# One transfer per group of ten query rows, on partitions 4 to 123, in an attention and two-layer MLP kernel

## The chip, the cores and the metric

The kernel runs on one core of a Trainium2 chip. The core has a matrix engine (PE, with its weight loads listed as PEld), a vector engine (DVE), a scalar engine (ACT), a general engine (POOL), a queue engine that here only issues transfers (SP), and 16 DMA engines that carry the transfers of all queues. On-chip memory (SBUF) and the matrix engine's result memory (PSUM) both have 128 partitions. The metric is the time of one execution in microseconds (us).

## The reference

Attention with two batches, 12 heads, 448 positions and 64 features per head, in which the heads are mixed before and after the softmax, and then two MLP layers on the 896 x 768 result:

```
scores = scale * q @ k^T
scores = einsum('bhij,hg->bgij', scores, w_pre)
attn = exp(scores - max(scores)) / (sum + 1e-9)
attn = einsum('bhij,hg->bgij', attn, w_post)
x = (attn @ v) laid out as [896, 768]
h = x @ w_in;  x = (h * relu6(h + 3) / 6) @ w_out
h = x @ w_in2; out = (max(h,0) + alpha * min(h,0)) @ w_out2
```

## The kernel before

Queries are cut into eight tiles of 120, 120, 120 and 88 rows per batch. For a tile, `qk` makes the scores of two heads at a time (`sc`), and `s_out` copies them to an SBUF tile `S` with query rows on the partitions and [head, key] along the free dimension. There are two such tiles, one for even and one for odd query tiles, so tile t can only be written once everything of tile t-2 has been read.

Mixing heads needs head and row together on the partitions. So the rows of a tile are taken in groups of ten (90 groups; in a 120-row tile group g has rows g, g+12, g+24, ..., in an 88-row tile the step is 8, and the last 8 rows are a group of their own). `pull` moves a group from `S` to a tile `pull` with 12 x 5 = 60 partitions per five rows: SBUF to SBUF, in pieces of 448 numbers (1792 bytes), one piece for each row and head. Before the change a group is moved by two transfers of five rows each, both to the same half of the partitions (0 to 59 for even groups, 64 to 123 for odd ones), beside each other in the free dimension. The scores lie with the first half of a tile's rows from partition 0 on and the second half from partition 64 on.

Two groups make a pair; there are 45 pairs, and the main loop runs over them. In iteration p: `premix(p)` multiplies the pulled rows with the block-diagonal `wpre` (PSUM tiles `mx`, two buffers) and takes the row maxima on DVE (`nm`); `qk` makes scores of a later tile; `exp(p)` runs on ACT; `s_out` copies the scores; `norm(p)` scales `wpost` on DVE; `post(p-1)` mixes the heads again on PE (`pt`), `post_evac(p-1)` copies the result to `MT` on ACT; `av` multiplies with the values for an earlier tile, and its result goes to `xT`. Near the end of the loop the first weight blocks are loaded and converted (`wst`, `wb`, `whi`, `wlo`) and the first chains of the MLP (`p`) begin.

All the instructions stand in the order of the program on each engine. SP issues, in iteration p, the pulls of the pair p+2 and the loads of queries, keys, values and weights. It waits only for what a transfer needs: the scores of a new tile, a free buffer (four pairs of `pull` tiles, two to four buffers of the others), and a semaphore of which there are eight for all transfers. It can therefore run ahead of the other engines by a pair or more.

From 254.8 us on there is only the MLP: 64 weight blocks, each used by 36 matmuls of 448 columns.

Of the kernel before, what the change touches and what calls it, by code (L numbers as in the profile page):

```python
# [7 lines left out]
F32 = mybir.dt.float32  # L8
# [7 lines left out]
PSUM = bass.MemoryType.PSUM  # L16

Q = 64
EB = 384

W_MIN = 2.0 ** -15
# [13 lines left out]
def kernel(  # L35
# [15 lines left out]
    nc = tc.nc  # L51
    _, D, H, S = k.shape
    B, D = q.shape[0], D // 2
    DM, NT = out.shape
    JP, NJ = v.shape[1], v.shape[3]
    JH = JP // 2
    KF = alpha.shape[0] // 128
    KD = DM // 128
    G = 10
    GP = G * H  # L60
    G2 = G // 2
    GH = G2 * H
    WP = GH
    HC = 3
    scale = 1.0 / float(D) ** 0.5

    tiles = []
    groups = []
    for b in range(B):
        for i0 in range(0, S, GP):  # L70
            n = min(GP, S - i0)
            t = len(tiles)
# [32 lines left out]
    with tc.manual_schedule():  # L105
# [21 lines left out]
        def load_q(ti, c):  # L127
            T = tiles[ti]
            n = T["n"]
            t = q_st[ti, c] = kq.tile([128, HC, GP], F32, tag="qst", bufs=4, name="qst")  # L130
            a = T["i0"] * H + 2 * HC * c * n
            for o in range(2):
                src = q[T["b"], D * o:D * o + D, a:a + 2 * HC * n]
                nc.sync.dma_start(  # L134
                    out=t[D * o:D * o + D, :, :n],
                    in_=src.rearrange("p (j o x) -> p j o x", j=HC, o=2)[:, :, o, :],
                )

# [7 lines left out]

        S_t, MT = {}, {}

        def half(ti):
            return G2 * (tiles[ti]["n"] // G)  # L150

        def qk(ti, j, tag="sc"):
            n, m = tiles[ti]["n"], half(ti)
            if j == 0:
                S_t[ti] = (s_odd if ti % 2 else s_even).tile([128, H, S], F32, tag="S", name="S")
            pool_ = psB if tag == "sc" else psA
            ps = [pool_.tile([128, 512], F32, tag=tag, bufs=2, name="sc") for _ in range(2)]
            t = q_st[ti, j // HC]
            for a, z, r in ((0, Q, 0), (m, n, Q)):
                for o in range(2):  # L160
                    nc.tensor.matmul(  # L161
                        ps[o][r:r + z - a, :S], t[D * o:D * o + D, j % HC, a:z],
                        k_st[tiles[ti]["b"]][D * o:D * o + D, j, :], start=True, stop=True,
                    )
            w = Q + n - m
            return [(S_t[ti][:w, 2 * j + o, :], ps[o][:w, :S]) for o in range(2)]

        d_t, mx_t, e_t, sm_t, wr_t, pt_t = {}, {}, {}, {}, {}, {}

        def pull(g):  # L170
            ti, o, st, xn = groups[g]
            if g % 2 == 0:
                d_t[g // 2] = late.tile([128, 2, S], F32, tag="pull", bufs=4, name="pull")
            r = Q * (g % 2)
            for c in range(2):
                x = min(G2, xn - c * G2)
                a = Q * c + o if st > 1 else Q + o - half(ti) + c * G2
                src = S_t[ti][bass.ds(a, x, step=st)] if st > 1 else S_t[ti][a:a + x]
                nc.sync.dma_start(d_t[g // 2][r:r + x * H, c, :], src)  # L179

        def premix(p):
            d = d_t.pop(p)
            ms = []
            for o in range(2):
                ms.append(psA.tile([128, 512], F32, tag="mx", bufs=2, name="mx"))
            for c in range(2):
                for o in range(2):
                    x = min(G2, groups[2 * p + o][3] - c * G2) * H
                    a = Q * o
                    nc.tensor.matmul(  # L190
                        ms[o][Q * c:Q * c + Q, :S], wpre[a:a + x], d[a:a + x, c, :],
                        start=True, stop=True,
                    )
            nms = []
            for m in ms:
                nm = late.tile([128, 1], F32, tag="nm", bufs=4, name="nm")
                nc.vector.tensor_reduce(nm, m[:, :S], axis=AX.X, op=ALU.max, negate=True)  # L197
                nms.append(nm)
            mx_t[p] = ms, nms
# [33 lines left out]

        def post_evac(p):
            ts = pt_t.pop(p)
            two = [groups[2 * p + o] for o in range(2)]
            for ti, *_ in two:
                if ti not in MT:
                    MT[ti] = late.tile([128, NJ, H, GP], F32, tag="MT", bufs=2, name="MT")
            for c in range(2):  # L240
                s = ts[c][:Q + JH, :2 * NJ * GH].rearrange("p (o u x) -> p u o x", o=2, x=G2)
                if two[0][0] == two[1][0] and two[1][2] > 1:
                    ti, o, _, _ = two[0]
                    d = MT[ti][:Q + JH, :, :, o * G:(o + 2) * G].rearrange("p t g (o x) -> p (t g) o x", o=2)
                    nc.scalar.copy(d[..., c * G2:(c + 1) * G2], s)  # L245
                    continue
                for k_, (ti, o, st, xn) in enumerate(two):
                    x = min(G2, xn - c * G2)
                    r = (o * G if st > 1 else o) + c * G2
                    d = MT[ti][:Q + JH].rearrange("p t g x -> p (t g) x")  # L250
                    nc.scalar.copy(d[:, :, r:r + x], s[:, :, k_, :x])

        def by_row(dst, src, n):
            m = n // G * G
# [145 lines left out]
        def open_late():  # L400
            p_late.close()
            p_xt.close()
            p_ps.close()
            P["ps6"] = pool(ctx, "ps6", bufs=6, space=PSUM)
            P["g1"] = pool(ctx, "g1", bufs=2 * KF - NE)
# [43 lines left out]
        def in_chain(i, xs, c):  # L449
            p = ptile()[:, :S]  # L450
            in_part(p, i, xs, c, 0, KD)
            return p

        def g_tile(f, c):
            return pair(P["g0" if c == 0 and f < NE else "g1"], "g")


        def act1(p, g, f):
            hi, lo = g
            t = P["tmp"].tile([128, S], F32, tag="t", name="t")  # L460
            nc.scalar.activation(out=t, in_=p, func=ACTF.Relu, bias=three)
            yield
            nc.vector.scalar_tensor_tensor(
                out=t, in0=t, scalar=6.0, in1=p, op0=ALU.min, op1=ALU.mult
            )
            nc.scalar.activation(out=hi, in_=t, func=ACTF.Copy, scale=1.0 / 6.0)
            yield
            nc.vector.scalar_tensor_tensor(
                out=lo, in0=t, scalar=1.0 / 6.0, in1=hi.bitcast(F32),
                op0=ALU.mult, op1=ALU.subtract,  # L470
            )
# [13 lines left out]
        def run(a):  # L485
            for _ in a:
                pass
# [28 lines left out]
        load_k0(3, H // 2)  # L516
        for c in range(2):
            a = GH * c
            nc.sync.dma_start(out=wpre[Q * c:Q * c + GH, :GH], in_=w_pre[a:a + GH, a:a + GH])
        load_q(1, 0)  # L520
        for c in range(2):
            a = GH * c
# [3 lines left out]
        nc.gpsimd.tensor_copy(  # L526
            wpost.rearrange("p (g x) -> p x g", g=H), wraw.rearrange("p (x g) -> p x g", g=H)
        )

        def s_out(pairs):  # L530
            for o, (d, s_) in enumerate(pairs):
# [46 lines left out]
        for p_ in range(-2, NP + 1):  # L578
            if p_ == -2:
                for g in range(4):  # L580
                    pull(g)
            elif 0 <= p_ < NP - 2:
                pull(2 * p_ + 4)
            for f in load_at.get(p_, []):
                f()
            for ti, c in load_q_at.get(p_, []):
                load_q(ti, c)
            if 0 <= p_ < NP:
                premix(p_)
            pend = [qk(ti, j, "mx" if p_ < 0 and j == 1 else "sc") for ti, j in qk_at.get(p_, [])]  # L590
            if 0 <= p_ < NP:
                exp(p_)
            for two in pend:
                s_out(two)
            if 0 <= p_ < NP - 2:
                pull(2 * p_ + 5)
            if 0 <= p_ < NP:
                norm(p_)
            if 1 <= p_:
                post(p_ - 1)  # L600
                post_evac(p_ - 1)
            kk = 2 * (p_ - (NP - KD // 2))
            if kk == 0:
                p0 = ptile()[:, :S]
            if 0 <= kk < KD:
                in_part(p0, 0, x_t, 0, kk, kk + 2)
            if p_ == NP:
                p1 = in_chain(1, x_t, 0)
                gs[0, 0] = g_tile(0, 0)
                run(act1(p0, gs[0, 0], 0))  # L610
                p2 = in_chain(2, x_t, 0)
                gs[1, 0] = g_tile(1, 0)
                run(act1(p1, gs[1, 0], 1))
            for f in also.get(2 * p_, []) + also.get(2 * p_ + 1, []):
                f()
            for ti, a in av_at.get(p_, []):
                av(ti, a)
# [2 lines left out]
                f()  # L620
        for a in range(H // 2):
            av(NTILE - 1, a)
        open_late()


# [138 lines left out]
```

## Time and profile before

| what | value |
|---|---|
| median of 3 runs | 713.36 us (710.69 to 714.17) |
| the profiled execution | 710.89 us, of which 709.1 us is the span from the first to the last instruction |
| PE busy | 671.9 us (95%) |
| DVE, ACT, POOL busy | 426.3, 359.4, 261.8 us |
| transfers on SP's queue | 33852 packets, 80.46 MB |
| mean granted clock of the matrix engine | 0.986 |

Busy time of PE counts a matmul from its start to its modelled end, also where several run beside each other in parts of the array, so a PE that reads as busy may still be short of work. The transfers of 1792 bytes are the pulls and the keys of the second batch.

### The profile page before, as it was taken

To read this page: it belongs to the slowest core of one execution; us is meant where nothing else is said; L and a number is where in the kernel's file an instruction comes from. 1 tells how busy PE (TensorE), PEld (TensorE's weight loads), DVE (VectorE), ACT (ScalarE), POOL (GpSimd) and SP (SyncE) were. 2 spreads that over 40 slices of the span, in tenths; PEclk is the share of its full clock that TensorE was granted. 3 is DMA by queue.
4 is the path that set the end of the run, shared out by engine and by line. 5 is a ranking of instruction groups with operands and counts; after the bars stand their busy time and mean duration, and the time that the engine had idled before them with its cause. 6 is when DMAs were issued, how large, how long until landed. Compare 5 with 4: busy or idle time off the path is not lost.

```text
span 709.1 us, 17560 instructions
## 1 busy us (share of the span) xinstructions
PE 671.9 (95%) x7464; PEld 567.8 (80%) x7464; DVE 426.3 (60%) x714; ACT 359.4 (51%) x672; POOL 261.8 (37%) x148
## 2 busy tenths in 40 slices
PE   6888989978888999999999999999999999999997
PEld 2445667746656889999999999999999999999997
DVE  3554666656552357888866454438999999535311
ACT  3554767766674556565654453344354344444310
POOL 0000000001133235545466646444555545776630
PEclk9999999999997899999999999999999999999999
DMA  4355433355424013232333323421322322445302
GB/s 137 137 166 154 137 131 100 129 184 169 151 72 145 7 47 133 90 124 100 109 115 134 133 96 127 133 91 54 125 90 97 125 90 90 145 156 191 122 0 79
DMA packets 34073, 81.80 MB, mean 115 GB/s; under 512 B 11468, under 2 KB 24652, under 8 KB 33996
## 3 DMA queue, kind: packets, MB, share of 16 engines
q1 hardware_dynamic: 33852, 80.46, 34.2%
q8 instruction: 59, 0.97, 0.6%
q10 hardware_dynamic: 144, 0.23, 0.1%
q14 instruction: 18, 0.15, 0.1%
HBM read 58.65 MB, written 2.75 MB: 87 GB/s over the span
## 4 chain that ended last, share of the span: by engine, by line
PE 70%; DMA 10%; SPq 7%; issue 4%; POOL 4%; ACT 3%; DVE 1%; POOLq 0%; DVEq 0%; ACTq 0%
PE p L441 58%; DMA pull<-S 10%; PE mx L190 4%; SPq L179 4%; PE pt L229 3%; PE av L275 3%; POOL wb L364 2%; PE sc L161 2%; POOL wlo L375 2%; SPq L134 2%; ACT e L206 1%; ACT MT L245 1%; SPq L142 1%; DVE nm L197 1%; DMA wraw<-in_w_post_dram 0%
## 5 line engine op out<-in xcount | busy, mean ns | idle before, releaser
L364 POOL TENSOR_TENSOR wb<-wb,wst 128x768 int32<-128x768 int32 x64 | 125.4, 1959 | 258.7 <-ACT xT L285 154.7
L375 POOL TENSOR_TENSOR wlo<-wb,whi 128x768 fp32r<-128x768 f32 x64 | 125.5, 1961 | 126.6 <-ACT whi L369 126.6
L441 PE MATMUL p<-xh,whi 128*128 128x448 f32 x384 | 140.7, 366 | 0.0
L441 PE MATMUL p<-xh,wlo 128*128 128x448 f32 x384 | 139.6, 364 | 0.0
L441 PE MATMUL p<-gh,whi 128*128 128x448 f32 x384 | 139.3, 363 | 0.0
L441 PE MATMUL p<-gh,wlo 128*128 128x448 f32 x384 | 138.9, 362 | 0.1
L441 PE MATMUL p<-xl,whi 128*128 128x448 f32 x384 | 138.9, 362 | 0.0
L441 PE MATMUL p<-gl,whi 128*128 128x448 f32 x384 | 138.7, 361 | 0.0
L190 PE MATMUL mx<-pull,wpre 60*64 60x448 f32 x360 | 92.2, 570 | 20.3 <-DMA pull<-S 15.5
L349 DVE TENSOR_SCALAR wb<-wb 128x768 f32<-128x768 f32 x64 | 51.0, 798 | 83.9 <-ACT wb L341 83.8
L341 ACT ACTIVATE wb<-wst 128x768 f32<-128x768 f32 x64 | 57.9, 904 | 73.1 <-DMA wst<-in_w_out_dram 54.6
L206 ACT ACTIVATE e<-mx,nm 128x448 f32<-128x448 f32 x90 | 56.5, 631 | 67.5 <-DVE nm L197 67.3
L197 DVE TENSOR_REDUCE nm<-mx 128x1 f32<-128x448 f32 x90 | 53.5, 620 | 50.7 <-PE mx L190 46.3
L229 PEld LDWEIGHTS pt<-wr,e 60*64 60x64 f32 (+1 forms) x2880 | 67.4, 137 | 16.0 <-issue 9.8
L369 ACT CAST whi<-wb 128x768 fp32r<-128x768 f32 x64 | 53.3, 833 | 48.0 <-PE p L441 29.8
L441 PEld LDWEIGHTS p<-xh,wlo 128*128 128x128 f32 x384 | 72.5, 189 | 5.7
L441 PEld LDWEIGHTS p<-gh,wlo 128*128 128x128 f32 x384 | 72.0, 187 | 5.9 <-POOL wlo L375 0.5
L441 PEld LDWEIGHTS p<-xl,whi 128*128 128x128 f32 x384 | 72.3, 188 | 5.1
L161 PE MATMUL sc<-kst,qst 64*64 64x448 f32 (+2 forms) x384 | 69.0, 579 | 7.4 <-DMA qst<-in_q_dram 3.9
L441 PEld LDWEIGHTS p<-xh,whi 128*128 128x128 f32 x384 | 72.4, 189 | 4.3
L441 PEld LDWEIGHTS p<-gh,whi 128*128 128x128 f32 x384 | 72.1, 188 | 4.6
L441 PEld LDWEIGHTS p<-gl,whi 128*128 128x128 f32 x384 | 71.9, 187 | 4.4
(46 smaller groups left out, 790.1 us busy)
## 6 DMA issues: line engine op xcount, KB each, us to landing
wst<-in_w_in_dram SPq DMA_DIRECT2D x32, 768.0 KB
wst<-in_w_out_dram SPq DMA_DIRECT2D x32, 768.0 KB
pull<-S SPq DMA_DIRECT2D x178, 105.0 KB
v<-in_v_dram SPq DMA_DIRECT2D x16, 168.0 KB
out_dram<-o SPq DMA_DIRECT2D x12, 224.0 KB
qst<-in_q_dram SPq DMA_DIRECT2D x24, 90.0 KB
kst<-in_k_dram SPq DMA_DIRECT2D x4, 336.0 KB
kst<-in_k_dram SPq DMA_DIRECT2D x1, 672.0 KB
```

The costliest lines, as they stand in the source:

```text
L161: nc.tensor.matmul(ps[o][r:r + z - a, :S], t[D * o:D * o + D, j % HC, a:z], k_st[tiles[ti]["b"]][D * o:D * o + D, j, :], start=True, stop= ...
L179: nc.sync.dma_start(d_t[g // 2][r:r + x * H, c, :], src)
L190: nc.tensor.matmul(ms[o][Q * c:Q * c + Q, :S], wpre[a:a + x], d[a:a + x, c, :], start=True, stop=True,)
L197: nc.vector.tensor_reduce(nm, m[:, :S], axis=AX.X, op=ALU.max, negate=True)
L206: nc.scalar.activation(out=e, in_=ms[o][:, :S], func=ACTF.Exp, bias=nms[o], accum_out=sm[:, o:o + 1])
L229: nc.tensor.matmul(ts[c][Q * z:Q * z + m, u:u + GH], e[a:a + GH, j:j + m], wr[a:a + GH], start=True, stop=True,)
L341: nc.scalar.activation(t, s[:, :, 1].bitcast(F32), ACTF.Abs)
L349: nc.vector.tensor_scalar(t, t, W_MAX, W_MIN, ALU.min, ALU.max)
L364: nc.gpsimd.tensor_tensor(n, n, st_t.pop(i)[:, :, 0].bitcast(I32), ALU.add)
L369: nc.scalar.copy(hi, b_t[i])
L375: nc.gpsimd.tensor_tensor(lo, b_t.pop(i), w_t[i][0].bitcast(F32), ALU.subtract)
L441: nc.tensor.matmul(p, wt[a], xt[c], start=(first and z == 0), stop=(last and z == 2))
```

## The change

A group's ten rows now come in one transfer. The tile `pull` has the two groups of a pair beside each other in the free dimension, and each group's 120 row-and-head pieces on the partitions 4 to 123, so that five rows end at partition 63 and five begin at 64. For that the scores lie on the partitions 4 to 123 without a gap at 64; the query tile gets four zero columns in front, and the four `pull` tiles are allocated once and have their first four partitions zeroed. `premix` runs over the partition halves (0 to 63 and 64 to 123) instead of over the groups, and `post_evac` copies a whole group at a time. Apart from that, the chain of the MLP's third block for the first batch (`p2`) and the activation of the second are moved behind the last `av`.

```
 Q = 64
+Z = 4
...
-            t = q_st[ti, c] = kq.tile([128, HC, GP], F32, tag="qst", bufs=4, name="qst")
+            t = q_st[ti, c] = kq.tile([128, Z + HC * GP], F32, tag="qst", bufs=4, name="qst")
+            nc.gpsimd.memset(t[:, :Z], 0.0)
...
-            for a, z, r in ((0, Q, 0), (m, n, Q)):
+            b, k_ = j % HC * n, k_st[tiles[ti]["b"]]
+            for a, z, r in ((b, b + Q, 0), (b + Q, b + Z + n, Q)):
                 for o in range(2):
                     nc.tensor.matmul(
-                        ps[o][r:r + z - a, :S], t[D * o:D * o + D, j % HC, a:z],
-                        k_st[tiles[ti]["b"]][D * o:D * o + D, j, :], start=True, stop=True,
+                        ps[o][r:r + z - a, :S], t[D * o:D * o + D, a:z], k_[D * o:D * o + D, j, :],
+                        start=True, stop=True,
                     )
...
         def pull(g):
             ti, o, st, xn = groups[g]
-            if g % 2 == 0:
-                d_t[g // 2] = late.tile([128, 2, S], F32, tag="pull", bufs=4, name="pull")
-            r = Q * (g % 2)
-            for c in range(2):
-                x = min(G2, xn - c * G2)
-                a = Q * c + o if st > 1 else Q + o - half(ti) + c * G2
-                src = S_t[ti][bass.ds(a, x, step=st)] if st > 1 else S_t[ti][a:a + x]
-                nc.sync.dma_start(d_t[g // 2][r:r + x * H, c, :], src)
+            d = d_buf[g // 2 % len(d_buf)]
+            src = S_t[ti][bass.ds(Z + o, xn, step=st)] if st > 1 else S_t[ti][Z + o:Z + o + xn]
+            nc.sync.dma_start(d[Z:Z + xn * H, g % 2, :], src)
...
             for c in range(2):
-                for o in range(2):
-                    x = min(G2, groups[2 * p + o][3] - c * G2) * H
-                    a = Q * o
+                for r in range(2):
+                    a, z = Q * r, Q + (groups[2 * p + c][3] - G2) * H if r else Q
                     nc.tensor.matmul(
-                        ms[o][Q * c:Q * c + Q, :S], wpre[a:a + x], d[a:a + x, c, :],
-                        start=True, stop=True,
+                        ms[r][Q * c:Q * c + Q, :S], wpre[a:z], d[a:z, c, :], start=True, stop=True
                     )
...
+                if xn == G:
+                    nc.scalar.copy(d[:, :, a:a + G].rearrange("p u (r x) -> p u r x", r=2), s)
                     continue
...
+        for _ in range(4):
+            d_buf.append(late.tile([128, 2, S], F32, tag=f"pull{len(d_buf)}", bufs=1, name="pull"))
+            nc.gpsimd.memset(d_buf[-1][:Z], 0.0)
...
-                p2 = in_chain(2, x_t, 0)
-                gs[1, 0] = g_tile(1, 0)
-                run(act1(p1, gs[1, 0], 1))
...
         for a in range(H // 2):
             av(NTILE - 1, a)
+        p2 = in_chain(2, x_t, 0)
+        gs[1, 0] = g_tile(1, 0)
+        run(act1(p1, gs[1, 0], 1))
```

On SP, early in the loop, these rows stood before (`qst` and `v` are loads of queries and values; rows alike are counted):

```order
L179 DMA pull<-S 60x1x448 x4
L142 DMA v_449<-in_v_dram 56x768 x2
L134 DMA qst<-in_q_dram 64x3x120 x2
L179 DMA pull<-S 60x1x448 x4
L142 DMA v_526<-in_v_dram 56x768 x2
L179 DMA pull<-S 60x1x448 x4
```

And the same place stands now so:

```order
L175 DMA pull<-S 120x1x448 x2
L144 DMA v_442<-in_v_dram 56x768 x2
L136 DMA qst<-in_q_dram 64x3x120 x2
L175 DMA pull<-S 120x1x448 x2
L144 DMA v_517<-in_v_dram 56x768 x2
L175 DMA pull<-S 120x1x448 x2
```

A pair takes two issues in place of four, each of 120 pieces in place of 60; the loads between them stay where they were.

On PE, at the end of the loop, the third chain (18 matmuls) stood directly behind the second, and the last `av` behind it:

```order
L441 MATMUL p<-xh,whi 128x448
L441 MATMUL p<-xl,whi 128x448
L441 MATMUL p<-xh,wlo 128x448
L275 MATMUL av<-MT,v_2498 64x88 x18
L275 MATMUL av<-MT,v_2591 64x88 x2
```

Now `av` comes first, and the third chain stands between it and the chains of the second batch:

```order
L266 MATMUL av<-MT,v_2612 64x88 x2
L266 MATMUL av<-MT,v_2683 64x88 x18
L432 MATMUL p<-xh,whi 128x448
L432 MATMUL p<-xl,whi 128x448
L432 MATMUL p<-xh,wlo 128x448
```

No matmul is added or removed there; only the place of the 18 has moved.

On POOL there are now small fills ahead of the first conversion of weights:

```order
L516 TENSOR_SCALAR wpre<-wpre 128x64
L517 COPY wpost<-wraw 128x5x12
L523 MEMSET pull 4x896 x4
L132 MEMSET qst 128x4 x11
L355 TENSOR_TENSOR wb<-wb,wst 128x768
L132 MEMSET qst 128x4
```

One fill of four columns has come in for every load of queries, and SP's load waits for it; the last one stands behind the first weight block's addition on POOL (`wb<-wb,wst`).

## Rows read from the trace of the kernel before

**Rows 1.** Windows: stretch, length, busy time by engine, granted clock, DMA share, GB/s.

```profile
20.00:201.50 181.50, 161.57 (x4156) 105.26 (x4152) 108.87 (x295) 117.29 (x296) 3.69 (x2) 0.99 0.45 143
201.50:254.80 53.30, 46.36 (x989) 36.06 (x986) 20.72 (x52) 28.98 (x71) 20.05 (x17) 0.84 0.24 69
254.80:709.10 454.30, 450.50 (x2251) 421.48 (x2250) 290.77 (x357) 206.88 (x294) 237.12 (x121) 1.00 0.32 109
```

**Rows 2.** The page's chain that ended last, shares of the span by line.

```profile
PE p L441 58%; DMA pull<-S 10%; PE mx L190 4%; SPq L179 4%; PE pt L229 3%; PE av L275 3%; POOL wb L364 2%; PE sc L161 2%; POOL wlo L375 2%; SPq L134 2%; ACT e L206 1%; ACT MT L245 1%; SPq L142 1%; DVE nm L197 1%; DMA wraw<-in_w_post_dram 0%
```

**Rows 3.** Timeline, DVE's row maxima of pairs 0, 17, 18, 39 and 44.

```profile
19.80 1.33 DVE L197 TENSOR_REDUCE nm<-mx 128x1 f32<-128x448 f32 x2 [3.28 <-PE mx L190]
...
100.37 1.16 DVE L197 TENSOR_REDUCE nm<-mx 128x1 f32<-128x448 f32 x2 [1.17 <-PE mx L190]
...
103.63 1.15 DVE L197 TENSOR_REDUCE nm<-mx 128x1 f32<-128x448 f32 x2 [0.35 <-PE mx L190]
...
201.51 1.15 DVE L197 TENSOR_REDUCE nm<-mx 128x1 f32<-128x448 f32 x2
...
236.19 1.16 DVE L197 TENSOR_REDUCE nm<-mx 128x1 f32<-128x448 f32 x2 [2.07 <-PE mx L190]
```

**Rows 4.** Timeline of SP's issues: start, length, count.

```profile
73.48 6.81 SPq L179 DMA_DIRECT2D pull<-S  x8
...
82.18 6.73 SPq L179 DMA_DIRECT2D pull<-S  x8
```

**Rows 5.** DMA view, window 86.5 to 88.5: packets; SP's queue with share of 16 engines.

```profile
DMA packets 152, 0.25 MB, mean 127 GB/s; under 512 B 10, under 2 KB 152, under 8 KB 152
...
q1 hardware_dynamic: 152, 0.25, 33.1%
```

**Rows 6.** The chain in order of time, 99.5 to 102.8: start, length, what.

```profile
99.50 0.75 PE mx L190 x8
100.25 0.75 PE sc L161 x8
101.00 0.93 PE pt L229 x64
101.93 0.83 PE av L275 x32
```

**Rows 7.** The chain, 192.6 to 197: ACT alone, in a pair with a weight block.

```profile
192.63 1.34 ACT e L206 x4
193.97 0.42 ACT S L532
194.39 1.01 ACT MT L245 x2
195.39 0.79 ACT wb L341
196.18 0.82 ACT wst L342
```

**Rows 8.** Windows in the tail of the loop, columns as in Rows 1.

```profile
214.60:224.90 10.30, 9.09 (x116) 6.72 (x120) 2.00 (x6) 4.12 (x9) 5.11 (x4) 0.50 0.30 86
...
231.70:238.50 6.80, 6.31 (x106) 5.47 (x107) 2.73 (x6) 2.52 (x8) 2.97 (x3) 0.50 0.00 0
```

**Rows 9.** DMA view, window 111 to 119 (pulls of an 88-row tile).

```profile
DMA packets 357, 0.63 MB, mean 79 GB/s; under 512 B 25, under 2 KB 354, under 8 KB 354
...
q1 hardware_dynamic: 354, 0.59, 27.7%
```

**Rows 10.** The chain: a transfer from issue to what it released, two places.

```profile
19.07 3.38 DMA pull<-S
...
61.59 8.20 DMA pull<-S
```

**Rows 11.** DMA view, window 222 to 225: last pulls beside the start of a weight load.

```profile
DMA packets 79, 0.18 MB, mean 61 GB/s; under 512 B 3, under 2 KB 68, under 8 KB 79
...
q1 hardware_dynamic: 79, 0.18, 36.8%
```

More of the change, by code (lines that the diff above doesn't have):

```diff
@@ L134, in load_q @@
                 nc.sync.dma_start(
-                    out=t[D * o:D * o + D, :, :n],
+                    out=t[D * o:D * o + D, Z:Z + HC * n].rearrange("p (j x) -> p j x", j=HC),
                     in_=src.rearrange("p (j o x) -> p j o x", j=HC, o=2)[:, :, o, :],
@@ L147 @@
         S_t, MT = {}, {}
-        def half(ti):
-            return G2 * (tiles[ti]["n"] // G)
         def qk(ti, j, tag="sc"):
-            n, m = tiles[ti]["n"], half(ti)
+            n = tiles[ti]["n"]
             if j == 0:
@@ L158, in qk @@
             t = q_st[ti, j // HC]
-            for a, z, r in ((0, Q, 0), (m, n, Q)):
+            b, k_ = j % HC * n, k_st[tiles[ti]["b"]]
+            for a, z, r in ((b, b + Q, 0), (b + Q, b + Z + n, Q)):
                 for o in range(2):
                     nc.tensor.matmul(
-                        ps[o][r:r + z - a, :S], t[D * o:D * o + D, j % HC, a:z],
-                        k_st[tiles[ti]["b"]][D * o:D * o + D, j, :], start=True, stop=True,
-                    )
-            w = Q + n - m
@@ L166, in qk @@
-            return [(S_t[ti][:w, 2 * j + o, :], ps[o][:w, :S]) for o in range(2)]
+                        ps[o][r:r + z - a, :S], t[D * o:D * o + D, a:z], k_[D * o:D * o + D, j, :],
+                        start=True, stop=True,
+                    )
+            return [(S_t[ti][:Z + n, 2 * j + o, :], ps[o][:Z + n, :S]) for o in range(2)]
         d_t, mx_t, e_t, sm_t, wr_t, pt_t = {}, {}, {}, {}, {}, {}
+        d_buf = []
         def pull(g):
             ti, o, st, xn = groups[g]
-            if g % 2 == 0:
-                d_t[g // 2] = late.tile([128, 2, S], F32, tag="pull", bufs=4, name="pull")
@@ L181, in premix @@
         def premix(p):
-            d = d_t.pop(p)
+            d = d_buf[p % len(d_buf)]
             ms = []
-            for o in range(2):
+            for r in range(2):
                 ms.append(psA.tile([128, 512], F32, tag="mx", bufs=2, name="mx"))
             for c in range(2):
-                for o in range(2):
-                    x = min(G2, groups[2 * p + o][3] - c * G2) * H
-                    a = Q * o
+                for r in range(2):
+                    a, z = Q * r, Q + (groups[2 * p + c][3] - G2) * H if r else Q
@@ L235, in post_evac @@
             ts = pt_t.pop(p)
-            two = [groups[2 * p + o] for o in range(2)]
-            for ti, *_ in two:
+            for c in range(2):
+                ti, o, st, xn = groups[2 * p + c]
                 if ti not in MT:
                     MT[ti] = late.tile([128, NJ, H, GP], F32, tag="MT", bufs=2, name="MT")
[L240 to L245, printed above, removed]
-                    continue
[L247 to L251, printed above, removed]
+                s = ts[c][:Q + JH, :2 * NJ * GH].rearrange("p (r u x) -> p u r x", r=2, x=G2)
+                a = o * G if st > 1 else o
+                d = MT[ti][:Q + JH].rearrange("p t g x -> p (t g) x")
+                if xn == G:
+                    nc.scalar.copy(d[:, :, a:a + G].rearrange("p u (r x) -> p u r x", r=2), s)
+                    continue
+                for r in range(2):
+                    x = min(G2, xn - r * G2)
+                    nc.scalar.copy(d[:, :, a + r * G2:a + r * G2 + x], s[:, :, r, :x])
         def by_row(dst, src, n):
@@ L518 @@
             a = GH * c
-            nc.sync.dma_start(out=wpre[Q * c:Q * c + GH, :GH], in_=w_pre[a:a + GH, a:a + GH])
+            nc.sync.dma_start(out=wpre[Z + GH * c:Z + GH * c + GH, :GH], in_=w_pre[a:a + GH, a:a + GH])
         load_q(1, 0)
```

## The prediction

> **What bounds the kernel now.** I read three stages first [rows 1]: the attention loop up to pair 38, the end of the loop, and the MLP from 254.8 us on. The MLP takes 454.3 us with PE busy for 450.5 of them, and the change adds nothing to it; so whatever is won or lost lies in the first 254.8 us. There, the chain that ended last is not PE alone: 10% of the whole span hangs on the transfer `pull<-S` and 4% on SP issuing it [rows 2], together some 100 us, all of them in the loop.
>
> The row maxima on DVE mark the pairs [rows 3]. Pair 0 starts at 19.80, pair 39 at 201.51: 39 pairs in 181.7 us, or 4.66 us a pair. But pairs 17 and 18 start only 3.26 us apart. What that pair consists of is seen in the chain at the same time [rows 6]: PE goes from `mx` (0.75) over `sc` (0.75) and `pt` (0.93) to `av` (0.83) without a break, which sums to 3.26. So 3.26 us is what PE needs when its data are there, and 1.4 us a pair is lost to something else.
>
> What that is, is shown by two views of the pulls. SP issues eight of them in 6.81 us and the next eight in 6.73 [rows 4], 0.85 us each: four a pair are 3.4 us, without the loads of queries, keys and values that stand in the same queue. And in a stretch with pulls alone, the 16 DMA engines are busy for 33.1% [rows 5]. That is 5.3 of 16. Its 152 packets are 10 tiny ones and 142 of 1792 bytes; 0.331 x 16 x 2 us = 10.6 us, or 75 ns a packet. A share that stands at 5 of 16 while SP has more to issue means that a pull is carried by about five engines, and its source has just five rows. 60 pieces over five engines are 12 each, 12 x 0.075 = 0.90 us, and four pulls a pair are 3.6 us of full use of these engines. With what the other loads add, both the queue and the five engines ask for more than PE's 3.26. When something else lies in the rings the pull is later still: one that took 3.38 us from issue to its effect at the start took 8.20 behind a load of keys [rows 10].
>
> **The change part by part.**
>
> *Half the issues.* 180 issues become 90. At 0.85 us [rows 4] a pair's cost on SP goes from 3.4 to 1.7 us. A new issue describes 120 pieces for 60; the trace has no such pull, so its cost is between 0.85 (nothing more) and 1.7 us (double). At double nothing is saved on SP, and SP alone would hold the pair near 3.4 plus the other loads. I take 0.85, since a pull differs from the old one in a count only, and keep the other for the range.
>
> *Ten rows in one transfer.* If the number of engines follows the rows of the source, as five engines for five rows suggest, ten carry the new one: 12 pieces each as before, 0.90 us a pull, but two a pair: 1.8 us in place of 3.6. The lower bound is that it stays with five engines, 24 pieces each: 3.6 us, nothing won. [...]
>
> With 1.7 us on SP and 1.8 us on the engines, both fall under PE's 3.26, and PE sets the pair. SP can then run ahead by up to the four pairs of `pull` buffers, so the new wait of each pull for the `premix` four pairs earlier ends long before.
>
> *What a pair then costs.* Pairs 0 to 38 at 3.26: 39 x 3.26 = 127.1. By the lists of the program one of them has two `qk` (+0.75) and five have two `av` (5 x 0.83 = 4.2); pairs with less work are not counted as shorter, since maxima, exponentials and the two `mx` buffers make a ring of about the same length. ACT alone needs 1.34 + 0.42 + 1.01 + 0.79 + 0.82 = 4.38 us in a pair with a weight block [rows 7], 1.1 more than PE; two such pairs are not covered by a second `av`: 2.2. Sum 134.3. At six changes of query tile the first pull still waits for the last copy of scores; four of these tiles begin with the second group of a pair, which leaves two pairs, 6.5 us, for an issue and a transfer that took 3.38 unladen [rows 10]: I allow 1 us each, 6 in all. 140 us against 181.7: **-41.5** (bounds: -47.4 with no allowance; the other end is the second rival).
>
> *Start.* Pair 0 needs two pulls in place of four: two issues less, 2 x 0.85, less 0.2 for a transfer that starts later on more pieces: **-1.5**.
>
> *The end of the loop.* From pair 39 to pair 44 the loop takes 236.19 - 201.51 = 34.7 us [rows 3]. [...] ACT has the most to do: casts of `xh` and `whi` ride on each pair, of the size of the two weight steps, so 4.38 us [rows 7] for five pairs are 21.9 us, 12.8 less. The rest up to 254.8 holds 2.3 us of half clock, worth 1.1. [...] I take **-10**, nearer to the full end, since in the loop before, where PE has work without a break, the clock is 0.99 [rows 1].
>
> *Costed at nothing.* The 16 fills of four columns on POOL: POOL was idle for all but 3.69 us of the first 181.5 [rows 1]; SP's load of queries now waits for its fill, and the last fill stands behind a weight addition on POOL; queued behind that load on SP are the pulls of two pairs ahead, so a delay under 3 us is covered and above that it shows one to one. `mx` and `sc` keep their number and columns. `post_evac` keeps its copies of 480 numbers. The 18 matmuls of `p2` move from before `av` to behind it on PE; they take the same time at both places, and `av` is ready at both, as `MT` is copied while the second chain runs.
>
> **A row that speaks against it.** In the 88-row tiles the pulls are slower already: 354 packets, 25 of them tiny, take 0.277 x 16 x 8 = 35.5 us, 100 ns each [rows 9] against 70 for the same mean in [rows 5]. [...] By the row alone, 24 pieces a pair at 0.107 (75 x 100/70) are 2.6 us, under 3.26. [...]
>
> **Sum.** -41.5 - 1.5 - 10 = -53. The profiled execution took 710.9 us (span 709.1 and 1.8 around it): 710.9 - 53 = **658 us**. The median of the runs shown is 2.5 above that execution, which is inside the range.
>
> **The rivals.**
>
> *The pulls still arrive late, behind other loads* (0.26). The excess of 8.20 over 3.38 is 4.8 us [rows 10], and came from a load of keys in the same rings, not from the five engines. Four loads of keys and three of weights lie in the loop: 7 x 4.8 = 34 us, and of the 53 only 19 would be won: 692 us; with two thirds of these delays 681. Against it: pulls can now be issued three pairs, 9.8 us, ahead. An issue at double cost ends in the same place.
>
> *The transfer stays on five engines* (0.05). Then a pair costs 3.6 us on the engines as before, and only SP gets free: 700 to 712 us. For it: nothing in this trace shows ten rows. Against it: five engines and five rows agree.
>
> *Slower: ten engines hinder each other* (0.04). [...] Beside a starting weight load 79 packets take 0.368 x 16 x 3 = 17.7 us, 0.22 us each [rows 11]. A pair has 24 pieces in a row in place of 48 of 75 ns; above 150 ns a piece the pair costs more than before. At 0.22 it would be 5.3 us for 3.6: 45 x 1.7 = 76 us, 787 us. Against it: in [rows 9] it is 0.1.
>
> *Better than forecast* (0.05): no loss at tile changes, and the full clock at the end: 710.9 - 47.4 - 1.5 - 14 = 648, and below that if pairs without `av` run shorter than 3.26.
>
> **How the numbers follow.** The forecast has 0.60, with its own range 645 to 672. The range for 8 in 10 leaves out the cases beyond 690: 645 to 690. What this measurement can tell from no change is about 0.5%, 3.6 us. Faster: forecast, better, late pulls and half of the five engines, 0.93; the same 0.03; slower 0.04.
>
> **What would show it.** Right: in windows with pulls alone the DMA share goes to 10 of 16 (0.62) in bursts, then falls, since SP waits; the mean over the loop stays near 0.45 x 181.5/140 = 0.58; pairs start 3.3 us apart; the chain has hardly any `pull<-S`; SP's issues stay near 0.8 us; the MLP takes 454 us, and it starts near 202. Wrong: a share that stays at 5 of 16; issues of 1.5 us; pairs that still take 4 us or more with the chain through the pulls around loads of keys or weights; a piece above 150 ns; a half clock that stays at the end.

## The result, and the profile after

The changed kernel takes **685.39 us** (median of 4 runs, 678.82 to 689.84), the kernel before 712.03 beside it. The ratio is 0.9595, 95% interval 0.9516 to 0.9674: faster by 4.0%, some 27 us. (The ratio is that of the means, without the run of 689.84, which counts as slow.) The forecast was 658 with a range of 645 to 690. So sign and range held, but half of the gain is missing.

The profiled execution took 685.79 us (span 684.0), against 710.9 for that of before: 25.1 us. First the stretches that answer to [rows 1], cut again at the start of pair 39 and where the MLP begins (columns as there).

```profile
20.00:186.80 166.80, 153.34 (x4156) 99.92 (x4158) 105.06 (x295) 113.98 (x291) 4.55 (x11) 1.00 0.51 153
186.80:230.00 43.20, 37.10 (x987) 30.50 (x978) 24.07 (x55) 28.95 (x71) 20.09 (x17) 1.00 0.38 102
230.00:684.00 454.00, 450.30 (x2251) 421.40 (x2249) 290.53 (x355) 206.53 (x291) 236.79 (x121) 1.00 0.31 107
```

The MLP is the same 454 us with PE busy for 450.3. All of the gain lies ahead of it: the loop to pair 39 went from 181.5 to 166.8 us, the rest from 53.3 to 43.2, with the granted clock there at 1.00 in place of 0.84. Next the page's chain that ended last, as [rows 2]:

```profile
PE p L432 59%; PE mx L185 4%; PE sc L161 4%; DMA pull<-S 4%; PE pt L223 4%; PE av L266 3%; ACT e L200 3%; POOL wb L355 2%; POOL wlo L366 2%; ACT MT L238 1%; DVE nm L191 1%; DMA kst<-in_k_dram 1%; DMA wst<-in_w_in_dram 1%; DVE xT L277 1%; ACT S L527 0%
```

`pull<-S` has gone from 10% to 4% and SP's issue of it is no longer among them, but the pulls are still there, and ACT's `e` has come up from 1% to 3%. The row maxima, as [rows 3], at pairs 0, 1, 39 and 44:

```profile
19.33 1.16 DVE L191 TENSOR_REDUCE nm<-mx 128x1 f32<-128x448 f32 x2 [2.34 <-PE mx L185]
22.43 1.16 DVE L191 TENSOR_REDUCE nm<-mx 128x1 f32<-128x448 f32 x2 [0.17 <-PE mx L185]
...
186.76 1.15 DVE L191 TENSOR_REDUCE nm<-mx 128x1 f32<-128x448 f32 x2
...
211.64 1.16 DVE L191 TENSOR_REDUCE nm<-mx 128x1 f32<-128x448 f32 x2 [0.50 <-PE mx L185]
```

Pair 0 starts 0.5 us earlier (1.5 forecast). Pairs 39 to 44 take 211.64 - 186.76 = 24.9 us in place of 34.7: -9.8, where -10 was forecast. Pairs 0 to 38 take 186.76 - 19.33 = 167.4 us in place of 181.7: **-14.3, where -41.5 was forecast**. Nearly the whole miss, 27 of 28 us, lies in this one term.

What the change was to do to the transfers, it does. SP's issues, as [rows 4], and two windows of the DMA view, as [rows 5], the first (24 to 26 us) in a tile that is read with a row step of 12, the second (88 to 90 us) in one with a step of 8, an 88-row tile:

```profile
14.55 5.90 SPq L175 DMA_DIRECT2D pull<-S  x7
```

```profile
DMA packets 282, 0.45 MB, mean 226 GB/s; under 512 B 33, under 2 KB 282, under 8 KB 282
...
q1 hardware_dynamic: 282, 0.45, 61.0%
```

```profile
DMA packets 140, 0.23 MB, mean 116 GB/s; under 512 B 10, under 2 KB 140, under 8 KB 140
...
q1 hardware_dynamic: 140, 0.23, 55.2%
```

An issue takes 0.84 us although it describes 120 pieces. In the first window 0.61 x 16 = 9.8 engines are busy, in 2 us with 282 packets: 69 ns each, as in [rows 5] (0.331 x 16 x 2 / 152 = 70, the tiny packets counted in). That is the 10 of 16 that the forecast asked for. In the second 0.552 x 16 x 2 = 17.7 us go to 140 packets, 126 ns each. The kernel before, in the same tile with five engines, has this from 96 to 98 us:

```profile
DMA packets 152, 0.25 MB, mean 126 GB/s; under 512 B 11, under 2 KB 152, under 8 KB 152
...
q1 hardware_dynamic: 152, 0.25, 32.9%
```

That is 69 ns, against 126 with ten engines; what makes the pieces longer is not shown. It cost no time: the chain has no transfer in it while the rows of the two tiles of this kind arrive and are mixed (82 to 112 and 185 to 215 us).

So the transfers cost less now, and still a pair takes 167.4 / 39 = 4.29 us and not 3.26. Three things are seen to hold it. First, the chain in order of time while the scores of an 88-row tile are made:

```profile
74.12 0.75 PE mx L185 x8
74.87 1.62 PE sc L161 x8
76.50 1.07 PE pt L223 x60
77.57 0.83 PE av L266 x32
```

Eight `sc` take 1.62 us where they take 0.75 in a 120-row tile [rows 6]. No late result is waited for; by line and form, over the whole run, the weight loads of the 28-column part stand still for 8.5 us, put down to "issue" (time in which the engine waited for nothing that the profile shows):

```profile
L161 PEld LDWEIGHTS sc<-kst,qst 64*28 64x28 f32 x48 | 1.6, 101 | 8.5 <-issue 8.5
```

The same view of the kernel before:

```profile
L161 PEld LDWEIGHTS sc<-kst,qst 64*48 64x48 f32 x48 | 4.8, 125 | 0.9 <-issue 0.6
```

The change made that part narrower: 92 - 64 = 28 columns in place of 48.

Second, the timeline of DVE and ACT between two pairs:

```profile
113.39 0.49 ACT L276 COPY xT<-av 128x360 f32<-128x360 f32 x1
...
113.91 0.53 DVE L277 TENSOR_TENSOR xT<-av,xT 128x360 f32<-128x360 f32 x1 [0.89 <-ACT xT L276]
...
114.36 1.15 DVE L191 TENSOR_REDUCE nm<-mx 128x1 f32<-128x448 f32 x2
```

Every third `av` is copied out, and VectorE's add stands ahead of the next pair's maxima: the pair takes 4.25 us. The trace of before has the same, in a pair of 4.31 us:

```profile
106.97 0.49 ACT L285 COPY xT<-av 128x360 f32<-128x360 f32 x1
...
107.49 0.53 DVE L286 TENSOR_TENSOR xT<-av,xT 128x360 f32<-128x360 f32 x1 [0.95 <-ACT xT L285]
...
107.94 1.14 DVE L197 TENSOR_REDUCE nm<-mx 128x1 f32<-128x448 f32 x2
```

Third, transfers behind loads, in the chain, as [rows 10], and the wait for a weight block:

```profile
140.07 8.10 DMA pull<-S
...
156.87 5.58 DMA wst<-in_w_in_dram
```

### The profile page after: what moved, and what is told of

It reads as the page before. It is cut to its first block, busy times and chain, and to the rows that moved or that the text cites. A ratio compares the mean times of both kernels' runs of the same rounds, so it can differ in the third digit from the quotient of the medians.

```text
span 684.0 us, 17507 instructions
## 1 busy us (share of the span) xinstructions
PE 653.9 (96%) x7464; PEld 556.6 (81%) x7464; DVE 426.1 (62%) x714; ACT 355.8 (52%) x664; POOL 265.8 (39%) x168
## 4 chain that ended last, share of the span: by engine, by line
PE 75%; ACT 6%; DMA 6%; issue 5%; POOL 4%; DVE 3%; SPq 1%; POOLq 0%; ACTq 0%
PE p L432 59%; PE mx L185 4%; PE sc L161 4%; DMA pull<-S 4%; PE pt L223 4%; PE av L266 3%; ACT e L200 3%; POOL wb L355 2%; POOL wlo L366 2%; ACT MT L238 1%; DVE nm L191 1%; DMA kst<-in_k_dram 1%; DMA wst<-in_w_in_dram 1%; DVE xT L277 1%; ACT S L527 0%
## 5 line engine op out<-in xcount | busy, mean ns | idle before, releaser
L432 PE MATMUL p<-xh,whi 128*128 128x448 f32 x384 | 138.8, 361 | 0.0
L360 ACT CAST whi<-wb 128x768 fp32r<-128x768 f32 x64 | 53.3, 832 | 50.2 <-PE p L432 32.0
L223 PEld LDWEIGHTS pt<-wr,e 60*64 60x64 f32 (+1 forms) x2880 | 57.4, 133 | 24.7 <-issue 12.3
L161 PE MATMUL sc<-kst,qst 64*64 64x448 f32 (+2 forms) x384 | 70.8, 557 | 6.9 <-DMA qst<-in_q_dram 4.0
L185 PE MATMUL mx<-pull,wpre 64*64 64x448 f32 (+1 forms) x360 | 63.3, 548 | 10.7 <-ACT e L200 5.1
L191 DVE TENSOR_REDUCE nm<-mx 128x1 f32<-128x448 f32 x90 | 51.9, 617 | 30.2 <-PE mx L185 30.2
```

The costliest lines, as they stand in the source:

```text
L161: nc.tensor.matmul(ps[o][r:r + z - a, :S], t[D * o:D * o + D, a:z], k_[D * o:D * o + D, j, :], start=True, stop=True,)
L185: nc.tensor.matmul(ms[r][Q * c:Q * c + Q, :S], wpre[a:z], d[a:z, c, :], start=True, stop=True)
L223: nc.tensor.matmul(ts[c][Q * z:Q * z + m, u:u + GH], e[a:a + GH, j:j + m], wr[a:a + GH], start=True, stop=True,)
L360: nc.scalar.copy(hi, b_t[i])
L432: nc.tensor.matmul(p, wt[a], xt[c], start=(first and z == 0), stop=(last and z == 2))
```

## The experiments

The theory after the result: the gain is that of the ten engines and the halved issues, and what is missing was hidden under the pulls or made by the new widths: (a) the 28-column part, (b) the add ahead of the maxima, (c) pulls behind loads. The rivals: the gain is not the transfers' at all but the layout's or the clock's; and the miss is (c) alone, as the first rival of the forecast has it. Medians, and ratios to the kernel before on the same chip beside them:

| run | edit on the changed kernel | us | ratio, 95% |
|---|---|---|---|
| a0_after | none | 684.56 | 0.9629, 0.9591 to 0.9667 |
| e1_wide | 48 columns again | 681.13 | 0.9572, 0.9538 to 0.9606 |
| e2_late | `xT` copy and add put off | 693.73 | 0.9736, 0.9697 to 0.9775 |
| e3_both | both | 691.04 | 0.9700, 0.9662 to 0.9738 |
| e4_five | two transfers of five rows | 708.42 | 0.9957, 0.9930 to 0.9984 |
| e5_cols | two transfers of ten rows, half the columns | 700.12 | 0.9838, 0.9806 to 0.9869 |
| e7_add | the add alone put off | 681.85 | 0.9591, 0.9551 to 0.9632 |
| e9_noload | second keys and values not loaded | 678.73 | 0.9550, 0.9512 to 0.9588 |
| e8_addwide | e1 and e7 | 679.46 | 0.9563, 0.9533 to 0.9592 |
| e12_pool | e8, loads on GpSimd's queue | 689.20 | 0.9689, 0.9653 to 0.9724 |
| e6_p2 | third chain back in its old place | 685.88 | 0.9638, 0.9612 to 0.9663 |
| e11_conv | e8, weight conversions behind `norm` | 680.62 | 0.9554, 0.9514 to 0.9595 |

Steps between the row maxima, from the profiled executions (us; the first row is where pair 0 starts):

| pairs | before | a0 | e1 | e4 | e5 | e7 | e9 | e8 | e11 |
|---|---|---|---|---|---|---|---|---|---|
| start | 19.80 | 19.48 | 19.56 | 20.41 | 23.03 | 21.07 | 19.28 | 18.95 | 21.02 |
| 13 | 3.68 | 4.09 | 3.14 | 4.62 | 3.85 | 4.28 | 4.03 | 3.58 | 3.58 |
| 18 | 4.31 | 4.24 | 4.25 | 4.25 | 4.25 | 3.26 | 4.25 | 3.26 | 3.26 |
| 30 | 7.37 | 6.47 | 8.78 | 8.13 | 6.87 | 7.75 | 5.52 | 9.19 | 10.01 |
| 34 | 8.33 | 7.66 | 8.15 | 8.49 | 7.86 | 6.88 | 7.45 | 7.54 | 9.23 |
| 0 to 38 | 181.7 | 163.1 | 160.3 | 183.8 | 176.2 | 159.5 | 157.3 | 158.7 | 156.9 |
| 30 to 38 | 46.7 | 43.9 | 44.6 | 49.6 | 44.9 | 43.7 | 42.7 | 45.7 | 46.0 |
| 39 to 43 | 34.7 | 26.5 | 26.6 | 29.5 | 27.1 | 25.9 | 27.2 | 26.2 | 27.6 |

**The changed kernel again.**

> The changed kernel once more, as the mark for the three beside it on this chip: 685 us, 679 to 690.

Measured 684.56. Its profiled execution has 163.1 us in pairs 0 to 38 and the first one 167.4, with the same span within 2 us: single sums of pairs differ by some 4 us from execution to execution, while a step such as that of pair 13 repeats (4.09 in both).

**Five rows a transfer.**

```diff
-            nc.sync.dma_start(d[Z:Z + xn * H, g % 2, :], src)
+            for i, x in ((0, G2), (G2, xn - G2)):
+                a, r = Z + o + i * st, Z + i * H
...
+                nc.sync.dma_start(d[r:r + x * H, g % 2, :], src)
```

> The change's layout (scores from partition 4, ring buffers, one row group of ten) stays, but each group's ten rows come in two transfers of five again, 60 pieces each. Theory: the gain comes from the transfers, ten engines and half the issues, so this falls back to within 6 us of the kernel before (705 to 718). Rival: the gain comes from the layout (fewer MT copies, other matmul widths) or from the clock; then it stays under 692.

Measured 708.42, 0.9957: nearly all of the gain is gone, with the layout kept. SP and the engines look as before [rows 4, 5]:

```profile
90.72 11.65 SPq L177 DMA_DIRECT2D pull<-S  x12
```

```profile
DMA packets 154, 0.25 MB, mean 125 GB/s; under 512 B 14, under 2 KB 154, under 8 KB 154
...
q1 hardware_dynamic: 154, 0.25, 32.8%
```

Twelve issues back to back at 0.97 us, and 5.2 engines of 16. The gain is the transfers'; the layout alone is worth some 3 us. The clock was not changed by itself: its median over the runs is 0.980 before, 0.9875 here and 0.9945 in a0, so part of what the transfers give may come through fewer stretches at half clock (2 x 0.020 x 709 = 28 us of them before, 2 x 0.0055 x 682 = 7.5 in a0, an estimate from the mean clock).

**Ten engines, but as many issues.**

```diff
-            nc.sync.dma_start(d[Z:Z + xn * H, g % 2, :], src)
+            for c in range(2):
+                w = slice(c * S // 2, (c + 1) * S // 2)
+                nc.sync.dma_start(d[Z:Z + xn * H, g % 2, w], src[:, :, w])
```

> Each group still comes in two transfers, but both of ten rows and half the columns (120 pieces of 896 bytes): ten engines take part, yet there are as many issues as before (4 a pair, some 0.8 us each, 3.2 us of SP against a pair of 3.1 to 3.3). If the engines taking part are what counts: 684 to 692. If the issues on SP count as much: 695 to 712, with SP's issues back to back for most of the first 200 us.

Measured 700.12: the issues count too, and for more. SP's issues, and two microseconds of the DMA view:

```profile
19.77 8.14 SPq L177 DMA_DIRECT2D pull<-S  x10
...
29.42 6.78 SPq L177 DMA_DIRECT2D pull<-S  x8
```

```profile
DMA packets 297, 0.24 MB, mean 120 GB/s; under 512 B 30, under 2 KB 297, under 8 KB 297
...
q1 hardware_dynamic: 297, 0.24, 35.1%
```

The pieces are half as long and take half the time (0.351 x 16 x 2 / 297 = 38 ns), so the engines have room; SP does not, at 0.8 us an issue and four a pair. From 708.4 to 700.1 is what ten engines give with the issues kept (8 us), although the pieces are twice as many; from there to 684.6 what half the issues and half the pieces give on top (16 us). That most of it is the issues is read from SP's rows above; five engines with half the issues were not tried. The chain of before [rows 2] had 10% for the transfers and 4% for issuing them, and would have ranked the two the other way.

**The narrow part made wide again.** Zeros fill 20 more columns of the query tile.

```diff
+            if n < GP:
+                nc.gpsimd.memset(t[:, Z + HC * n:Z + HC * n + 20], 0.0)
...
-            for a, z, r in ((b, b + Q, 0), (b + Q, b + Z + n, Q)):
+            for a, z, r in ((b, b + Q, 0), (b + Q, b + max(Z + n, Q + 48), Q)):
```

> In 88-row tiles the second query part is 48 columns wide again (28 with the change); 20 more columns are read and their results not used. Theory A (the 28-column matmuls do not run beside the 64-column ones: eight sc take 1.6 us in place of 0.75, in twelve of the 42 steps of the loop): sc of these tiles returns to 0.75, 12 x 0.85 = 10 us less, 675. Theory B (the longer sc lies under the ring of maxima and exponentials or under late pulls): sc gets shorter, the time stays within 3 us of the changed kernel.

Measured 681.13, 3.4 us less, a third of the expected, and the interval still touches that of a0. The mechanism shows in the chain of such a tile:

```profile
66.24 0.38 PE mx L187 x4
66.62 0.69 PE sc L163 x7
67.31 0.92 PE pt L225 x59
68.22 0.88 PE av L268 x32
```

`sc` is back at 0.7 us, and pair 13 at 3.14. Part of it was given back elsewhere: pair 16 took 7.69 us in place of 6.07, and pair 30, which waits for a transfer of 7.98 us, 8.78 in place of 6.47.

**The copy-out put off.** First the copy and the add together, behind the next pair's exponentials:

> The copy and the addition that take the attention result from PSUM stand behind the exponentials of the next pair, not ahead of its row maxima. Theory A (each of them holds the next row maxima up by 1.1 us, and PE is not the bound in these pairs): eleven to twelve pairs 1.1 us shorter, 673. Theory B (PE or late pulls set the pair, DVE only seems to): within 3 us of the changed kernel.

> Both edits. Theory A: the two savings lie in different pairs and add, 663. If one of them is covered by the other, about 673; if late pulls are what holds the loop, 680 or more.

Measured 693.73 and 691.04: 9 and 6 us slower than the changed kernel, which neither theory of the first had. The waits of the first of them say why:

```profile
PEld av L273 <- ACT xT L284: 8.7, 8, 1.7
...
PE av L273 <- ACT xT L284: 7.5, 7, 1.6
```

In the changed kernel these two are 2.4 and 2.0 us. Pair 18 did fall from 4.24 to 3.27, but `av` has two PSUM buffers, and later `av` wait until they are copied out. So the add alone, with the copy left where it is:

```diff
...
                     nc.scalar.copy(d, s0)
-                    nc.vector.tensor_tensor(d, s1, d, ALU.add)
+                    x_adds.append(lambda d=d, s1=s1: nc.vector.tensor_tensor(d, s1, d, ALU.add))
...
                 premix(p_)
+            flush()
```

> Only VectorE's add into xT is put off, to behind the next pair's row maxima; ScalarE's copy stays where it is, so that the two av buffers come free about 1 us later and not 3. Theory: the add ahead of the maxima is what makes pairs 9, 18, 20, 22, 31 and 33 take 4.25 us in place of 3.15 to 3.26; they fall to 3.3 and the time to 673 to 679 (11 such pairs at 1.1 us, some of it lost to late transfers). Rival: the copy on ScalarE ahead of the exponentials costs as much, or the av buffers wait as when both were put off: 682 to 690.

Measured 681.85, just under the rival's 682 to 690, and its interval touches that of a0. Pairs 18, 20 and 22 are at 3.26 to 3.43, so (b) is right as a mechanism, but it is worth 3 us and not the 6 to 12 expected: pair 21 rose from 3.14 to 4.39, and the pull that ends pair 30's wait takes 8.82 us from its issue in place of 7.41.

**No second keys and values.** The first sequence's are used for both.

> Leaves out the loads of the second sequence's keys and values (8 transfers in the loop); the first sequence's are used for both. Theory, the rival of the prediction that transfers of scores come late behind other loads: pairs 10 to 12, 16 and 30, which take 5 to 8 us with a transfer behind a load ending last in their chain, fall to 3.2 to 4.3, and the time by 8 to 14 us to 671 to 677. If these pairs are held by something else (eight score matmuls of 1.6 us, the ring of buffers) the time stays within 3 us of 684.6.

Measured 678.73, 5.8 us less: below the 8 to 14 expected. Pair 10 fell from 4.34 to 3.25 and pair 12 from 5.24 to 4.52, but pair 30 only to 5.52 and pair 16 not at all. The loads of the first weights and of the queries are still there. With these transfers out of the way, another chain takes the place: pair 28, where a0 waits for a pull of 3.92 us, is now

```profile
126.61 0.62 DVE nm L191
...
127.31 1.34 ACT e L200 x4
128.66 0.42 ACT S L527
129.08 0.93 ACT MT L238 x2
130.01 0.26 ACT xT L276
130.29 0.50 DVE xT L277 x2
130.79 0.54 DVE nm L191
```

One pair through ACT and DVE is 4.2 us, without a transfer and without PE. Pair 30's 5.52 us are of the same kind, with the first weight block's conversions between (1.01 us on ACT, 0.57 and 0.56 on DVE).

**Both edits, and where the rest sits.**

> Two of the costs found one by one are taken away together: the second score part of the 88-row tiles is 48 columns wide again (alone 3.4 us faster) and VectorE's add into xT stands behind the next pair's row maxima (alone 2.7 us faster). If they are separate: 677 to 680, with pairs 9 to 14, 18, 20 and 22 all at 3.1 to 3.5 us. If what they free is taken back by transfers of scores that land late, as pairs 30 and 43 of each showed: 680 to 684.

Measured 679.46: 3.4 us alone and 2.7 alone give 5.1 together. Of the pairs named, 9, 18, 20 and 22 came to 3.26 to 3.50 us, but 10 to 14 stay at 3.58 to 4.11. It is, by median, the fastest of the versions that leave nothing out. The intervals against the kernel before (0.9533 to 0.9592, and 0.9591 to 0.9667 for a0) meet at their ends, but all six of its runs (677.54 to 683.41) lie below all six of a0 (684.03 to 690.82).

What the two edits free may be partly lost again in the clock. Windows around pair 30 of this kernel, columns as in [rows 1]; the pull ahead of them landed 8.41 us after its issue at 130.95:

```profile
135.00:140.00 5.00, 1.83 (x18) 0.56 (x14) 1.12 (x2) 2.10 (x3) 0.00 (x0) 0.81 0.75 196
140.00:145.00 5.00, 5.00 (x100) 3.50 (x96) 3.32 (x8) 2.41 (x7) 0.00 (x0) 0.50 0.51 184
145.00:150.00 5.00, 5.00 (x142) 4.20 (x140) 3.00 (x9) 3.54 (x9) 1.94 (x3) 1.00 0.01 3
```

TensorE is busy for 1.83 of 5 us while that pull is out; then it works without a break, but the granted clock is 0.50 for all of 140 to 145 us. Over the span it is 0.987 here and 0.995 in a0's profiled execution: 2 x 0.013 x 677.5 = 17.6 us at half clock against 6.8, an estimate from the mean. But over its six runs the clock goes from 0.987 to 0.997, and the run at 0.997 took 678.65 us, hardly less than the 679.32 of this one; what the clock takes back is not shown.

Then its loads of keys, values and the first three weights on another queue:

```diff
...
-                nc.sync.dma_start(
+                nc.gpsimd.dma_start(
                     out=t[Q * a:Q * a + JH], in_=v[b, JH * a:JH * a + JH, HC * c:HC * (c + 1)]
...
```

> As the kernel with both edits, but the loads of keys, values and the first three weights are issued on GpSimd's queue and not on SP's, so that a transfer of scores does not stand behind them on one queue. Rival of the late transfers: pairs 16, 24, 28, 30, 34 and 43, where a transfer behind a load ends last, lose 1 to 4 us each, and the time falls by 6 to 12 us to 667 to 674. If the transfers share the DMA engines with the loads whatever the queue: within 3 us of the kernel with both edits.

Measured 689.2, 10 us slower. GpSimd, which is idle, issues the first values and then keys one behind the other at once, and in the chain a pull issued behind the first of them takes 16 us:

```profile
15.16 2.32 POOL L146 DMA_DIRECT2D v<-in_v_dram  x4
...
17.51 2.06 POOL L146 DMA_DIRECT2D v<-in_v_dram  x4
```

```profile
19.11 16.05 DMA pull<-S
```

Pair 0 starts at 27.19 us and takes 9.80 to the next. So this run does not tell whether a queue of its own would help a pull later on: pair 30 still took 10.08, pair 34 5.16 and not 7.54. It shows that SP's order had been holding these loads back.

The weight conversions, moved to where TensorE does the post mixing:

```diff
...
-                at(a + 3 + z, lambda f=f, i=i: f(i))
+                mid.setdefault((a + 3 + z) // 2, []).append(lambda f=f, i=i: f(i))
...
```

> As the kernel with both edits, but the conversions of the first three weights stand directly behind norm, while TensorE works on the post mixing, and no longer ahead of the next pair's exponentials and row maxima. Theory: these conversions (ScalarE's wb and wst at 0.8 us each, VectorE's three at 0.5 to 1.0) hold pairs 34, 36 and 37, which take 7.5, 4.1 and 5.3 us in all variants; they fall to 3.3 to 4.5 each and the time to 671 to 676. Rival: pair 34 waits for the weight's transfer, which waits for its only buffer; then ScalarE waits there as long, and the time stays at 677 to 681.

Measured 680.62, no difference. The rival came true: pair 37 fell from 5.32 to 4.40, but pair 34 rose from 7.54 to 9.23, since ACT now stands in the conversion until its block is there:

```profile
149.78 5.58 DMA wst<-in_w_in_dram
...
156.17 0.86 ACT wst L343
157.03 0.93 ACT MT L240 x2
```

**The moved chain of the first layer.**

> The changed kernel, but the third chain of the first layer and its activation stand again where they did before the change, ahead of the last av. The prediction costed this move at nothing: within 2 us of the changed kernel (683 to 687). Rival: it gave some of the 10 us at the end of the loop; then 3 us or more are lost, behind pair 44.

Measured 685.88, 1.3 us from the changed kernel, with intervals that lie over each other: no worth of the move is seen, as costed.

## Why the prediction was right in sign and half wrong in size

- *The bound.* Right. Putting the five-row transfers back (e4) takes 24 of the 27 us away again. In the order e4, e5, a0 the engines give 8 of them, and half the issues and pieces 16.
- *Half the issues; ten rows in one transfer.* Both right: 0.84 us an issue, 9.8 engines, pieces of 69 ns. In the 88-row tiles the pieces took nearly twice as long (126 ns against 69), and no time was lost by it. The row against it [rows 9] was misread: of its six issues two are the tile's last group, eight rows side by side, and four are the next tile's; with a step of 8 five engines took 69 ns and not 100.
- *What a pair then costs: pairs 0 to 38 at 3.26, 140 us.* **The step that failed**, by 27 us. It took the pair at 100.37, one of the shortest, as the price of all, and put the 1.4 us above it down to the pulls as a whole. But pairs 18, 20 and 37 of the kernel before already took 4.31, 4.30 and 5.92 us with no transfer of a pull in the chain over them, and they hardly changed (4.25, 4.25 and 6.12). Where it is missing is plain: pairs 30 to 38 took 46.7 us before and 44.3 after (43.9 in a0), where nine times 3.26 is 29.3. The pair with two `qk`, 16, was to cost 3.26 + 0.75 and takes 6.08, as its second `qk` stands 2.1 us until DVE has copied scores out of PSUM. Taken away one at a time, the add ahead of the maxima was worth 2.7 us by the medians (e7), the narrow part 3.4 (e1), neither clear of the noise alone; the two together 5.1 (e8) and loads of keys and values 5.8 (e9), both clear. If these last two add, which was not tried, they are 11 of the 23 to 27 us missing. In e8 pairs 0 to 29 take 113.0 us and pairs 30 to 38 45.7, where 39 times 3.26 would give 97.8 and 29.3. Half of what is left is thus in nine pairs around the first weight blocks, where a pull behind loads (pair 30), a block's transfer (34) and ACT's and DVE's own work (37) stand one behind the other.
- *Costed at nothing: "`mx` and `sc` keep their number and columns".* Wrong for `sc`: 48 columns became 28, 8.5 us of standing still on the weight loads, of which some 3 showed in the time. In the changed kernel 144 loads of 64x60 beside 64x64 ones wait 3.4 us in all, 48 of 64x28 wait 8.5; in e8 48 of 64x48 wait 0.0 (0.9 in the kernel before). What the narrow loads stand still for is not shown; the runs show only that 48 columns do away with it.
- *The start.* -0.5 for -1.5: the sign right, the size within a microsecond.
- *The end of the loop.* Right in size, -9.8 for -10 (-8.1 in a0). The -10 was the author's estimate, under the 12.8 + 1.1 = 13.9 that [rows 7] and the end of [rows 8] give (236.19 to 238.5 us at a granted clock of 0.50); no run shows more than the 9.8. But with five-row transfers (e4) these pairs take 29.5 us, so about half of it does not hang on the pulls, and what gives that half was not separated. The half clock of [rows 8] (0.50) is gone in this execution (1.00 from 186.8 to 230 us); that of a0 had some again (0.73 from 205 to 210 us), and its pairs took 26.5 us.
- *The rivals.* Pulls late behind other loads came true in part: 5.8 us by e9, where the rival had 23 to 34 us (e9 keeps the loads of weights). That its 681 to 692 fits the measured time is luck: it gave the time for only a part of the reason. Of the rival with ten engines that hinder each other, longer pieces came in one kind of tile (126 ns against 69) and cost nothing there. The measured time also lies in the range of 645 to 690 only because the range was made wide for this rival; the forecast's own was 645 to 672.
- *Open.* How the last 16 us of pairs 30 to 38, and more than half of the miss as a whole, divide was not settled: e11 and e12 moved the waits and did not remove them. A second buffer for the early weight blocks was not tried.

## What to carry to other kernels

A chain's share is what a resource costs with everything behind it still hidden. Before a gain is counted as so many pairs down to the shortest pair, read each pair's step and take the floor from those that the resource does not touch; here pairs 18, 20 and 37 of the old trace showed that many pairs have another. A change of layout also changes the shape of matmuls at the edges: list the forms before and after by line. And a wait removed at one place was paid for here at the next scarce buffer (two `av` buffers in PSUM, where `av` waited 8.7 and 7.5 us in e2 for 2.4 and 2.0 in a0; one weight buffer, where pair 34 took 9.23 us in e11 for 7.54 in e8), so moving one operation by one step (e7, 681.85 us) did better than moving two further (e2, 693.73 us).

## What the runs showed of the hardware

- An issue on SP took 0.81 to 0.85 us in stretches back to back, whether the transfer had 60 pieces of 1792 bytes [rows 4], 120 of 1792 (the changed kernel) or 120 of 896 (e5); in one stretch of twelve with 60 pieces it took 0.97 (e4). Half as many issues, with half as many pieces, were worth 16 us here (e5 to a0).
- Pieces of 1792 bytes took 69 to 75 ns [rows 5], of 896 bytes 38 ns (e5), and in an 88-row tile, read with a row step of 8, with ten engines 126 ns (the changed kernel), where with five engines they took 69 (the kernel before).
- After 5 us in which TensorE was busy for 1.83, a pull being out for 8.41, the granted clock stood at 0.50 for the next 5 us with TensorE busy throughout (e8).
- Weight loads of 28 columns among ones of 64 stood still 0.71 us each time they began (8.5 us over 12 times, the changed kernel); of 48 columns 0.0 to 0.9 us in all over 12 times (e8 and the kernel before).
